# GpSimd's unread write behind every second scatter of x, two small steps on ScalarE, and new places in a fused attention and expert kernel

## The chip, the cores and the metric

One core of one Trainium2 chip. The metric is the device time of one execution, in microseconds (us), as the median of several runs. Engines are named as in the profile: PE (TensorE's matmuls), PEld (its weight loads), DVE (VectorE), ACT (ScalarE), POOL (GpSimd), SP (SyncE, which issues most of the DMAs).

## What is computed

An attention over channels, then a layer of experts over its output. Cut to what matters:

```python
# q, k, v: (4, 5056, 256); attention between the 256 channels of a batch
qn = q / (norm(q, axis=1) + 1e-06)
kn = k / (norm(k, axis=1) + 1e-06)
a = softmax(kn.transpose(0, 2, 1) @ qn / tau)        # (4, 256, 256)
x = (v @ a).reshape(20224, 256)
# experts: tokens with x @ w_skip > 0 go to the expert with the largest logit
e_idx = argmax(xc @ w_gate); gate_w = softmax(xc @ w_gate)[e_idx]      # 8 experts
y[mask_e] = gate_w * (relu(xc[mask_e] @ w1[e]) @ w2[e])                # 256 -> 1024 -> 256
out = x;  out[do_compute] = xc + y
```

## The kernel before

The tokens of a batch are cut into 4 chunks of 1280 (10 groups of 128), so there are 16 chunks, numbered c or d from 0 to 15. The work of one TensorE runs through these stages, which overlap:

- **Scores** (`scores`, L734, matmul L743): for chunk c, ten steps that add `k^T q` of 128 tokens into a PSUM tile of the batch. Meanwhile ScalarE squares q and k (L714) and VectorE adds the squares up (`add_squares`, L718) for the norms. The `qk` tiles are loaded in halves of a chunk, with 5 buffers.
- **Softmax** (`softmax`, L746), once a batch, behind its fourth chunk of scores: copy of the sums, norms by matmuls with ones (L730), square root, reciprocal, exponent (L772), then `aug` = exponent x 1 / sum (L778, VectorE), transposes of `aug` on TensorE (L783), the product with the gate's weights (L791), and the split of `aug` into `aH` and `aL` (L797, L799).
- **Product** (`attend`, L803, matmuls L815 to L817): for chunk d, five steps of two groups each into one of two pairs of PSUM banks (`px`). ScalarE copies each step out (`keep_x`, L821): `xo` (L824) holds x, `lg` (L825) holds the ten logits. `xo` has three buffers (`NXO`), so the first copy of chunk d waits until the scatters and the store of chunk d - 3 have landed.
- **Routing** (`route`, L839) of chunk d, from `lg`: maximum and difference (VectorE), exponent (`r_ex`, L853, ScalarE), the one-hot of the expert and its running count (L856 to L865, VectorE), the counts per partition as `r_rc` (L868, VectorE), two matmuls that sum them over the partitions (L871, L872, TensorE), `r_before` (L875, ScalarE), then offsets and places (`r_off` L883 to `r_posi` L894, VectorE). `base` carries the counts from chunk to chunk.
- **Scatter** (L897, GpSimd): ten indirect DMAs a chunk, each writing 128 rows of `xo` (x, token number, gate weight) to their places in `srt`, a list in DRAM sorted by expert. Behind each stands `pace` (L648): a memset of a tile `idle` that nothing reads (L650). The scatters of all chunks form one chain in GpSimd's order. `end_lists` (L657) closes the lists with four more scatters (L671) that have no memset between them.
- **First experts** (`first_ahead`, `second_ahead`): 7 blocks of 512 tokens of one expert, from the scatters of the first 6 chunks (`D0`), multiplied between and behind the products of the last chunks. `xs` and `xg` are their rows, loaded from `srt`; `put_ahead` scatters the result to `out` (L236, GpSimd).
- **Small slots** (`Small.part`), one after the other with the rest of the first experts, then two loops over what is left (`Large.loop`, L460; `Small.loop`, L602), whose code is no part of the change. The loop of large slots runs from about 502 us to the end.

The order of every engine up to the loops is made by a planner (`Plan`, L61): each step is a task with an engine, a cost, dependencies and a due time. Due times come from a table, `PLACES` (L51): two numbers for each chunk of scores (A), each chunk of products (B), each block of first experts (H) and each small slot (S). `run` (L109) hands due times back along the dependencies, simulates the engines and sorts the tasks by start; the program is written out in that order, and each engine keeps it. Costs are numbers such as `("G", 3.5)`: GpSimd's two scatters with their memsets.

Of the kernel before, what the change touches and what calls it, by code (L numbers as in the profile page):

```python
# [48 lines left out]
NXO = 3  # L49

PLACES = """  # L51
A0 89.87 855.42, A1 390.44 1819.31, A2 -81.94 1047.65, A3 -59.52 1015.95, A4 -190.99 1534.08, A5 -120.99 1138.75, A6 499.15 783.13, A7 799.47 1506.97, 
A8 1050.89 1421.23, A9 298.20 825.70, A10 1109.61 1383.20, A11 632.60 1820.36, A12 403.39 543.02, A13 425.18 1096.75, A14 1034.62 1129.27, A15 429.61 1087.73, 
B0 1339.22 1377.19, B1 -184.38 1551.63, B2 716.25 1563.50, B3 81.23 1352.19, B4 1080.02 1305.66, B5 743.88 863.60, B6 558.44 1600.08, B7 1608.33 1676.51, 
B8 288.55 958.87, B9 -0.98 1608.03, B10 259.38 1309.95, B11 174.32 789.24, B12 1048.96 1138.93, B13 919.54 2739.02, B14 949.98 1651.89, B15 178.90 1291.75, 
H0 672.92 1892.93, H1 231.51 1144.86, H2 169.77 1607.46, H3 1140.58 1342.54, H4 671.59 905.84, H5 257.88 1165.77, H6 1054.77 1575.39, S0 517.30 1920.36, 
S1 491.32 1739.07, S2 822.24 1425.79, S3 270.07 987.21, S4 568.78 659.45, S5 1154.04 1192.59, S6 1621.29 1716.68, S7 1357.86 1445.79
"""


class Plan:  # L61
# [18 lines left out]
    def chain(self, gen, *steps, deps=(), due=1e9):  # L80

        ts = []
        for engine, cost in steps:
            ts.append(self.add(engine, cost, lambda: next(gen, None), [*deps, *ts[-1:]], due))
            deps = ()
        return ts
# [90 lines left out]
def attn_moe(ctx: ExitStack, tc: tile.TileContext, q_k, vt, tau, w_skip, w_gate, w1, w1q, w2, out):  # L177
# [470 lines left out]
    def pace():  # L648

        G.memset(idle, 0.0)  # L650
# [95 lines left out]
    def softmax(b):  # L746


        u = pb.tile([P, 2, C], F32, name="u")
        S.copy(u, sums[b])  # L750
        yield
        add_norms(b)
        yield
        m = norms[b]
        nrm = pb.tile([P, C + 4], F32, name="nrm")
        V.tensor_scalar(nrm, m[:, : C + 4], 1e-30, None, ALU.max)
        yield
        S.activation(nrm, nrm, AF.Sqrt)
        yield
        V.tensor_scalar(nrm, nrm, 1e-6, None, ALU.add)  # L760
        V.reciprocal(nrm, nrm)
        rk = pb.tile([P, 2], F32, name="rk")
        V.tensor_scalar(rk, nrm[:, C : C + 4 : 2], itau, None, ALU.mult)
        yield
        mx = pb.tile([P, 2], F32, name="mx")
        den = pb.tile([P, 2], F32, name="den")
        for cb in range(2):
            V.scalar_tensor_tensor(u[:, cb, :], u[:, cb, :], rk[:, cb : cb + 1], nrm[:, :C], ALU.mult, ALU.mult)
        V.tensor_reduce(mx, u, AX.X, ALU.max, negate=True)
        yield  # L770
        for cb in range(2):
            S.activation(u[:, cb, :], u[:, cb, :], AF.Exp, bias=mx[:, cb : cb + 1], accum_out=den[:, cb : cb + 1])  # L772
        yield
        V.tensor_scalar(den, den, 1e-9, None, ALU.add)
        V.reciprocal(den, den)
        aug = pb.tile([P, 2, NA], F32, name="aug")
        for cb in range(2):
            V.tensor_scalar(aug[:, cb, :C], u[:, cb, :], den[:, cb : cb + 1], None, ALU.mult)  # L778
        yield
        pt = ps_m.tile([P, 2, C], F32, name="m")  # L780
        for cb in range(2):
            for kb in range(2):
                T.transpose(pt[:, kb, cb * P : (cb + 1) * P], aug[:, cb, kb * P : (kb + 1) * P], ident)  # L783
        yield
        aT = u
        S.copy(aT, pt)
        yield
        pw = ps_m.tile([P, 512], F32, name="m")
        for cb in range(2):
            for kb in range(2):  # L790
                T.matmul(pw[:, cb * 10 : cb * 10 + 10], aT[:, kb, cb * P : (cb + 1) * P], w9[:, kb, :], start=(kb == 0), stop=(kb == 1), skip_group_check=True)  # L791
        yield
        V.tensor_copy(aug[:, :, C:], pw[:, :20].rearrange("p (c e) -> p c e", c=2))
        yield
        aH = pb.tile([P, 2, NA], F32R, name="aH", bufs=2)
        aL = pb.tile([P, 2, NA], F32R, name="aL", bufs=2)
        S.copy(aH, aug)  # L797
        yield
        V.tensor_tensor(aL, aug, aH, ALU.subtract)  # L799
        augs[b] = (aH, aL)  # L800
        yield
# [37 lines left out]
    def route(d):  # L839
# [25 lines left out]
        V.tensor_tensor_scan(inc, segm, oh.rearrange("p e t -> p (e t)"), 0.0, ALU.mult, ALU.add)  # L865
        inc = inc.rearrange("p (e t) -> p e t", e=E)
        rc = tile_([P, E], "r_rc", F32R)
        V.tensor_copy(rc, inc[:, :, n - 1 : n].rearrange("p e o -> p (e o)"))  # L868
        yield
        m = ps_m.tile([P, 512], F32, name="m")  # L870
        T.matmul(m[:, :E], tri_r, rc, start=True, stop=True, skip_group_check=True)  # L871
# [24 lines left out]
        for t in range(n):  # L896
            i = G.indirect_dma_start(  # L897
                out=srt, out_offset=IndirectOffsetOnAxis(ap=posi[:, t : t + 1], axis=0),
                in_=xos[d][:, t, :], in_offset=None, bounds_check=E * CAP - 1, oob_is_err=False)
            in_list(i)  # L900
            if d >= D0:
                beside(i, "later lists", "first lists")
            else:
                first_listed.append(i.ins.name)
            pace()
            if t % 2:
                yield

    def tables(start):
# [83 lines left out]
    for c in range(NC):  # L993
        b, ch = divmod(c, NCH)
        ld, users = {}, ([], [])
        for h in range(2):
            cuts = {(0, 0): (0, 1, 2, 3, 4, JH), (0, 1): (0, 2, JH), (1, 0): (0, 2, JH)}.get((c, h), (0, JH))
            for j0, j1 in zip(cuts, cuts[1:]):
                t = then("qk", add("D", 0.68 * (j1 - j0), lambda c=c, h=h, j0=j0, j1=j1: load_qk(c, h, j0, j1), due=1e9 if c else -99, hold=("part", 99) if j0 else ("qk", NQ)))
                t.users = [] if j0 else users[h]  # L1000
                ld.update((h * JH + j, t) for j in range(j0, j1))
        for n in range(2):
            for h in range(2):
                begins = ch == 0 and h == 0
                s0 = then(("sq", n), add("S", 1.18, lambda c=c, n=n, h=h: squares(c, n, h), [ld[j] for j in range(h * JH, (h + 1) * JH)], hold=None if begins else ("sqh", 3)))
                users[h].append(s0)
                if begins:
                    if b:
                        s0.deps.append(ready_a[b - 1, "n"])
                    summed[n] = s0  # L1010
                else:
                    summed[n] = add("V", 1.41, lambda c=c, n=n, h=h: add_squares(c, n, h), [s0, summed[n]])
                    s0.users = [summed[n]]
            if ch == NCH - 1:
                summed[n] = add("V", 1.53, lambda n=n: fold_squares(n), [summed[n]])
        g = scores(c)
        for j in range(J):
            deps = [ld[j]]
            if j == 0 and ch == 0 and b > 1:
                deps.append(freed_s[b - 2])  # L1020
            t = then("A", add("T", 0.865, lambda g=g: next(g), deps, at("A", c, j)))
            if j % JH == JH - 1:
                users[j // JH].append(t)
        last_a = t
        if c == 2:
            third = t
        if ch == NCH - 1:
            g = softmax(b)
            s0, = chain(g, ("S", 0.5), deps=[t])
            n0, = chain(g, ("T", 0.8), deps=[s0, summed[0], summed[1]])  # L1030
            s = chain(g, ("V", 0.36), ("S", 1.65), ("V", 2.3), ("V", 1.55), ("S", 2.35), ("V", 0.97), deps=[n0])
            m0, = chain(g, ("T", 0.45), deps=s[-1:])
            m1, = chain(g, ("S", 0.5), deps=[m0])
            m2, = chain(g, ("T", 0.9), deps=[m1])
            m3, = chain(g, ("V", 0.12), deps=[m2])
            aH, = chain(g, ("S", 0.55), deps=[m3])
            aL, = chain(g, ("V", 0.65), deps=[aH])
            m0.hold = m2.hold = ("m", 1)
            m0.users, m2.users = [m1], [m3]
            freed_s[b], ready_a[b], ready_a[b, "n"] = s0, aL, n0  # L1040
            if b:
                s0.deps.append(ready_a[b - 1])
            norms_read = s[0]
# [8 lines left out]
    for d in range(NC):  # L1052
# [22 lines left out]
        stored[d] = then("st", add("D", 3.4, lambda d=d: store(d), [s], at("B", d, 4, by=16.5)))  # L1075
        g = route(d)
        r = chain(g, ("V", 0.43), deps=[s] + ([routed[d - 1]] if d else []))
        r += chain(g, ("S", 0.17), ("V", 1.02), ("V", 0.46), deps=r)
        rt, = chain(g, ("T", 0.22), deps=r[-1:])
        ra, = chain(g, ("S", 0.07), deps=[rt])  # L1080
        rt.hold, rt.users = ("m", 1), [ra]
# [1 line left out]
        routed[d], = chain(g, ("V", 0.51), deps=[based[d]])  # L1083
        routed[d].due = at("B", d, 4, by=2)
        s0.users = [routed[d]]
        in_order["sc"] = chain(g, *[("G", 3.5)] * (J // 2), deps=[routed[d], in_order.get("sc")], due=at("B", d, 4, by=15 if d < D0 else 45))[-1]
        sorted_[d] = plan.landed(in_order["sc"], 4.3)
        if d == NC - 1:
            g = end_lists()
# [202 lines left out]
```

## Time and profile before

| | |
|---|---|
| median of 3 runs | 778.78 us (778.5 to 779.02) |
| the profiled execution | 777.67 us |
| its span, first to last instruction | 775.9 us |
| TensorE busy in the span | 740.7 us |
| VectorE, ScalarE, GpSimd busy | 519.7, 346.8, 369.9 us |
| mean granted clock of TensorE | 0.986 |

The profiled execution is one run with its own time; its rows give durations and waits, and the span is 1.8 us shorter than its time. In the page, a matmul's end is modelled, so an engine that is shown busy may hold short waits. The idle time of an engine matters only where a later step of the bounding engine waits for it. In rows of groups, "x160 | 189.0, 1181 | 102.3 <-..." is: how many, busy us in all, mean ns of one, idle us before them and what ended it.

### The profile page before, as it was taken

The page shows a single profiled execution, that of the slowest core. Times are in us where ns is not written, and L with a number is a line of the kernel's source. Part 1 is how long each engine was busy: PE and PEld are TensorE (multiplying, and loading weights), DVE is VectorE, ACT ScalarE, POOL GpSimd, SP SyncE. Part 2 cuts the span into 40 slices and gives each one's busy share as a digit, 9 for nine tenths or more (in the row PEclk, how much of TensorE's full clock was granted, in tenths as well). Part 3 has the DMA queues.
Part 4 walks back from the last instruction along what each step waited for, and adds up shares of the span by engine and source line. Part 5 has one row for each costly group of instructions (what it writes and reads, how often), then busy time and mean ns, then how long its engine had stood idle before and what let it go on. Part 6 is the DMA issues. An engine that isn't in the chain of part 4 may idle for free. (4 is left out here: it accounts for less than half of the span.)

```text
span 775.9 us, 13511 instructions
## 1 busy us (share of the span) xinstructions
PE 740.7 (95%) x4352; PEld 643.9 (83%) x4352; DVE 519.7 (67%) x995; ACT 346.8 (45%) x605; POOL 369.9 (48%) x450
## 2 busy tenths in 40 slices
PE   9989999698999699999997999999999999999996
PEld 8879998698988688899886677788888888888885
DVE  3877959695887597777983425266657576666755
ACT  4678648545863655343230314143434243434422
POOL 1000899999999998889864130311122211111122
PEclk9999999899999899999999999999999999999998
DMA  8999998799958737466369996252533425152441
GB/s 323 398 390 342 357 353 289 259 333 378 353 194 238 213 116 230 134 218 161 132 216 296 305 382 234 79 184 75 167 97 108 135 73 178 60 183 75 129 117 54
DMA packets 97651, 165.98 MB, mean 214 GB/s; under 512 B 50650, under 2 KB 75460, under 8 KB 89280
## 3 DMA queue, kind: packets, MB, share of 16 engines
q1 hardware_dynamic: 85136, 144.03, 55.8%
q0 software_dynamic: 11776, 21.31, 7.9%
q8 instruction: 26, 0.43, 0.2%
q14 instruction: 25, 0.20, 0.1%
q10 hardware_dynamic: 688, 0.01, 0.0%
HBM read 122.26 MB, written 53.92 MB: 227 GB/s over the span
## 5 line engine op out<-in xcount | busy, mean ns | idle before, releaser
L897 POOL DMA_INDIRECT srt<-xo,r_posi x160 | 189.0, 1181 | 102.3 <-ACT sqh L714 73.5
L236 POOL DMA_INDIRECT out<-xg x76 | 76.1, 1001 | 251.9 <-DVE xg L371 227.4
L743 PE MATMUL s<-qk 128*128 128x256 f32 x640 | 146.8, 382 | 2.6 <-DMA qk<-in_qk 2.6
L743 PEld LDWEIGHTS s<-qk 128*128 128x128 f32 x640 | 118.9, 191 | 18.2 <-DMA qk<-in_qk 3.8
L815 PE MATMUL px<-aH,vH 128*128 128x266 f32 x320 | 98.7, 309 | 14.8 <-ACT lg L825 14.6
L344 DVE SCALAR_TENSOR_TENSOR hL<-ph,hH 128x512 fp32r<-128x512 f32 x96 | 66.4, 691 | 58.9 <-ACT hH L343 57.6
L343 ACT ACTIVATE hH<-ph 128x512 fp32r<-128x512 f32 x96 | 57.4, 598 | 98.0 <-PE ph L340 98.0
L816 PE MATMUL px<-aL,vH 128*128 128x266 f32 x320 | 92.9, 290 | 0.9 <-DVE aL L799 0.9
L817 PE MATMUL px<-aH,vL 128*128 128x266 f32 x320 | 92.7, 290 | 0.0
L650 POOL MEMSET none<- 128x512 bf16 x160 | 88.7, 554 | 0.0
L363 PE MATMUL po<-w2s,hH 128*128 128x512 f32 x336 | 83.8, 391 | 0.0
L824 ACT COPY xo<-px 128x512 f32<-128x512 f32 x80 | 47.2, 591 | 69.8 <-PE px L817 36.9
L815 PEld LDWEIGHTS px<-aH,vH 128*128 128x128 f32 x320 | 61.8, 193 | 17.3 <-ACT lg L825 16.2
L338 PE MATMUL ph<-xH,w1H 128*128 128x512 f32 x192 | 74.9, 390 | 0.9 <-PE m L1175 0.9
L339 PE MATMUL ph<-xL,w1H 128*128 128x512 f32 x192 | 74.8, 390 | 0.0
L340 PE MATMUL ph<-xH,w1L 128*128 128x512 f32 x192 | 74.7, 389 | 0.0
L714 ACT ACTIVATE sqh<-qk 128x1280 f32<-128x1280 f32 x56 | 69.3, 1273 | 9.2 <-DMA qk<-in_qk 4.8
L363 PEld LDWEIGHTS po<-w2s,hH 128*128 128x128 f32 x336 | 61.2, 189 | 11.5
L307 ACT CAST xH<-xt 128x512 fp32r<-128x512 f32 x40 | 24.9, 623 | 90.4 <-DVE xt L305 90.4
L816 PEld LDWEIGHTS px<-aL,vH 128*128 128x128 f32 x320 | 62.0, 194 | 2.3 <-DVE aL L799 1.4
L371 DVE SCALAR_TENSOR_TENSOR xg<-po,xg 128x256 f32<-128x256 f32 x90 | 43.5, 483 | 30.1 <-PE po L365 28.6
L817 PEld LDWEIGHTS px<-aH,vL 128*128 128x128 f32 x320 | 61.6, 192 | 0.0
(184 smaller groups left out, 1351.1 us busy)
## 6 DMA issues: line engine op xcount, KB each, us to landing
qk<-in_qk SPq DMA_DIRECT2D x29, 1280.0 KB
vf<-in_vt SPq DMA_DIRECT2D x32, 640.0 KB
out<-xo SPq DMA_DIRECT2D x12, 1280.0 KB
xg<-srt SPq DMA_DIRECT2D x20, 516.0 KB, 3.3
xs<-srt SPq DMA_DIRECT2D x80, 128.0 KB, 3.2
v1r<-in_w SPq DMA_DIRECT2D x10, 1024.0 KB
v2r<-in_w SPq DMA_DIRECT2D x10, 1024.0 KB
w1r<-in_w1q SPq DMA_DIRECT2D x8, 1024.0 KB, 5.5
```

What stands on the lines that cost most here:

```text
L236: i = (G.indirect_dma_start(out=out, out_offset=IndirectOffsetOnAxis(ap=ls, axis=0), in_=src, in_offset=None, bounds_check=NTOK - 1, oob_i ...
L338: T.matmul(ph, self.w1H[:, fs], self.xH[:, kb, :], start=(kb == 0), stop=False)
L339: T.matmul(ph, self.w1H[:, fs], self.xL[:, kb, :], start=False, stop=False)
L340: T.matmul(ph, self.w1L[:, fs], self.xH[:, kb, :], start=False, stop=(kb == 1))
L363: yield T.matmul(po, self.hH[:, f, ts], self.w2s[:, f, :, :], start=(f == 0), stop=False, skip_group_check=True)
L650: G.memset(idle, 0.0)
L714: S.activation(to, qk[c, h][:, n], AF.Square)
L743: T.matmul(sums[b][:, cb, :], kt[:, j % JH, cb * P : (cb + 1) * P], qt[:, j % JH, :], start=(ch == 0 and j == 0 and cb == 0), stop=(ch == ...
L815: T.matmul(px[:, i, :NA], vH[:, kb, js], aH[:, kb, :], start=(kb == 0), stop=False)
L816: T.matmul(px[:, i, :NA], vH[:, kb, js], aL[:, kb, :], start=False, stop=False)
L817: T.matmul(px[:, i, :NA], vL[:, kb, js], aH[:, kb, :], start=False, stop=(kb == 1))
L897: i = G.indirect_dma_start(out=srt, out_offset=IndirectOffsetOnAxis(ap=posi[:, t : t + 1], axis=0), in_=xos[d][:, t, :], in_offset=None, b ...
```

## The change

`pace()` moves inside the test for every second scatter, so that a chunk of ten scatters has five memsets. In `route`, `r_rc` is copied by ScalarE and not by VectorE. In `softmax`, the two multiplications that make `aug` run on ScalarE (an activation with a scale for each partition) and not on VectorE. Each of the two steps becomes a task of its own, with a cost in the planner, and the cost of GpSimd's pair of scatters goes from 3.5 to 3.4. The 47 pairs of `PLACES` are all new; their numbers are due times and say little one by one.

```diff
 PLACES = """
-A0 89.87 855.42, A1 390.44 1819.31, A2 -81.94 1047.65, A3 -59.52 1015.95, A4 -190.99 1534.08, A5 -120.99 1138.75, A6 499.15 783.13, A7 799.47 1506.97, 
...
+A0 -212.84 779.51, A1 1321.85 2287.98, A2 1288.02 1918.41, A3 921.83 1283.14, A4 -211.85 1066.57, A5 1.96 1135.44, A6 1521.56 1748.04, A7 866.77 2427.61, 
...
@@ softmax
         V.reciprocal(den, den)
+        yield
         aug = pb.tile([P, 2, NA], F32, name="aug")
         for cb in range(2):
-            V.tensor_scalar(aug[:, cb, :C], u[:, cb, :], den[:, cb : cb + 1], None, ALU.mult)
+            S.activation(aug[:, cb, :C], u[:, cb, :], AF.Copy, scale=den[:, cb : cb + 1])
@@ route
         rc = tile_([P, E], "r_rc", F32R)
-        V.tensor_copy(rc, inc[:, :, n - 1 : n].rearrange("p e o -> p (e o)"))
+        yield
+        S.copy(rc, inc[:, :, n - 1 : n].rearrange("p e o -> p (e o)"))
...
-            pace()
             if t % 2:
+                pace()
                 yield
@@ costs in the planner
-            s = chain(g, ("V", 0.36), ("S", 1.65), ("V", 2.3), ("V", 1.55), ("S", 2.35), ("V", 0.97), deps=[n0])
+            s = chain(g, ("V", 0.36), ("S", 1.65), ("V", 2.3), ("V", 1.55), ("S", 2.35), ("V", 0.35), ("S", 0.75), deps=[n0])
-        r += chain(g, ("S", 0.17), ("V", 1.02), ("V", 0.46), deps=r)
+        r += chain(g, ("S", 0.17), ("V", 1.02), ("V", 0.33), ("S", 0.18), deps=r)
-        in_order["sc"] = chain(g, *[("G", 3.5)] * (J // 2), deps=[routed[d], in_order.get("sc")], due=at("B", d, 4, by=15 if d < D0 else 45))[-1]
+        in_order["sc"] = chain(g, *[("G", 3.4)] * (J // 2), deps=[routed[d], in_order.get("sc")], due=at("B", d, 4, by=15 if d < D0 else 45))[-1]
```

Lines behind the changed ones move down by one to two (L897 becomes L899, L824 becomes L825, L853 becomes L854, L875 becomes L877; `r_rc` is L870, `aug` L779). Two places of the order follow; numbers behind a name tell one buffer's use from another.

GpSimd, at the end of the chain of scatters, where the last rows of chunk 15 are followed by the closing scatters. Before:

```order
L650 MEMSET none_143 128x512
L897 DMA srt_88<-xo_3753,r_posi_4077 167424x258
L650 MEMSET none_143 128x512
L668 CAST endi_4213<-ends_4209 128x4
L671 DMA srt_88<-none_143,endi_4213 167424x258 x4
```

Now:

```order
L650 MEMSET none_143 128x512
L899 DMA srt_88<-xo_3755,r_posi_4004 167424x258 x2
L650 MEMSET none_143 128x512
L668 CAST endi_4137<-ends_4133 128x4
L671 DMA srt_88<-none_143,endi_4137 167424x258 x4
```

Scatters stand in pairs with one memset behind them. The closing scatters stand without one, as before.

ScalarE, from the last product step of chunk 4 to the first of chunk 5, which is the first copy into the `xo` buffer that chunk 2 held. Before (`xo_1369` is chunk 5, `r_ex_1387` and `r_before_1463` are the routing of chunk 4):

```order
L824 COPY xo_1241<-px_1331 128x2x256
L825 COPY lg_1271<-px_1331 128x20
L700 CAST vH_1365<-vf_1163 128x1280
L714 ACTIVATE sqh_1388<-qk_1029 128x1280
L853 ACTIVATE r_ex_1387<-r_d_1385 128x80
L824 COPY xo_1369<-px_1370 128x2x256
L825 COPY lg_1406<-px_1370 128x20
L824 COPY xo_1369<-px_1392 128x2x256
L825 COPY lg_1406<-px_1392 128x20
L714 ACTIVATE sqh_1444<-qk_1188 128x1280
L875 COPY r_before_1463<-m_1447 128x16
```

Now (`xo_1441` is chunk 5; `r_ex_1388`, `r_rc_1414` and `r_before_1439` are the routing of chunk 4):

```order
L825 COPY xo_1268<-px_1359 128x2x256
L826 COPY lg_1289<-px_1359 128x20
L700 CAST vH_1382<-vf_1126 128x1280
L854 ACTIVATE r_ex_1388<-r_d_1386 128x80
L714 ACTIVATE sqh_1400<-qk_1191 128x1280
L714 ACTIVATE sqh_1410<-qk_1191 128x1280
L870 CAST r_rc_1414<-r_inc_1412 128x8
L714 ACTIVATE sqh_1429<-qk_1238 128x1280
L877 COPY r_before_1439<-m_1431 128x16
L714 ACTIVATE sqh_1464<-qk_1238 128x1280
L825 COPY xo_1441<-px_1442 128x2x256
L826 COPY lg_1470<-px_1442 128x20
```

All three ScalarE steps of the routing of chunk 4 now stand ahead of the first copy of chunk 5; before, `r_before` stood behind it.

## Rows read from the trace of the kernel before

**Rows 1.** The page, part 1: busy us, share of the span, instructions.

```profile
PE 740.7 (95%) x4352; PEld 643.9 (83%) x4352; DVE 519.7 (67%) x995; ACT 346.8 (45%) x605; POOL 369.9 (48%) x450
```

**Rows 2.** The waits, whole span: who waited for whom, us in total, times, longest.

```profile
ACT xo L824 <- DMA srt<-xo,r_posi: 31.7, 7, 7.4
...
PE px L815 <- ACT lg L825: 14.6, 4, 6.7
...
PE px L338 <- DVE xg L371: 4.3, 1, 4.3
```

**Rows 3.** The timeline of PE: start, us, instruction, idle before it and what ended it.

```profile
145.79 0.59 PE L815 MATMUL px<-aH,vH 128*128 128x266 f32 x1 [6.00 <-ACT lg L825]
...
265.56 0.59 PE L815 MATMUL px<-aH,vH 128*128 128x266 f32 x1 [6.70 <-ACT lg L825]
```

**Rows 4.** The timeline of ACT at the same two places.

```profile
145.07 0.59 ACT L824 COPY xo<-px 128x512 f32<-128x512 f32 x1 [6.25 <-DMA srt<-xo,r_posi]
...
264.84 0.59 ACT L824 COPY xo<-px 128x512 f32<-128x512 f32 x1 [6.13 <-DMA srt<-xo,r_posi]
```

**Rows 5.** The timeline of POOL: scatters of chunks 2, 4, 8 and 9.

```profile
129.58 2.10 POOL L897 DMA_INDIRECT srt<-xo,r_posi  x1 [0.17 <-issue]
...
137.68 0.98 POOL L897 DMA_INDIRECT srt<-xo,r_posi  x1 [0.17 <-DVE r_mx L848]
...
159.61 0.97 POOL L897 DMA_INDIRECT srt<-xo,r_posi  x1 [0.16 <-ACT sqh L714]
...
257.91 0.97 POOL L897 DMA_INDIRECT srt<-xo,r_posi  x1 [0.16 <-DVE xt L305]
...
259.59 0.99 POOL L897 DMA_INDIRECT srt<-xo,r_posi  x1 [0.17 <-issue]
```

**Rows 6.** Windows: us, busy us of PE, PEld, DVE, ACT, POOL, granted clock, DMA share, GB/s.

```profile
78.00:259.00 181.00, 169.83 (x1038) 155.65 (x1036) 140.69 (x286) 111.36 (x193) 165.93 (x180) 0.98 0.86 305
```

**Rows 7.** Windows, line L650 (the unread write) alone: us, busy POOL.

```profile
78.00:259.00 181.00, 49.52 (x90) 0.98 0.86 305
```

**Rows 8.** Windows, line L897 (the scatters) alone: chunk 2, and chunks 0 to 8.

```profile
116.00:139.00 23.00, 16.29 (x10) 1.00 0.84 272
78.00:259.00 181.00, 117.64 (x90) 0.98 0.86 305
```

**Rows 9.** The timeline of DVE: two adds, two steps of chunk 4's routing.

```profile
129.35 1.48 DVE L718 TENSOR_TENSOR sqk<-sqk,sqh 128x1280 f32<-128x1280 f32 x1
...
137.88 1.48 DVE L705 TENSOR_TENSOR vL<-vf,vH 128x1280 fp32r<-128x1280 f32 x1
...
149.27 0.17 DVE L883 TENSOR_TENSOR r_off<-r_before,base 128x8 f32<-128x8 f32 x1 [5.63 <-ACT r_before L875]
...
150.52 0.17 DVE L894 SCALAR_TENSOR_TENSOR r_posi<-r_pos,r_mx 128x10 int32<-128x10 f32 x1
```

**Rows 10.** The timeline of POOL: the closing scatters.

```profile
397.16 0.99 POOL L671 DMA_INDIRECT srt<-none,endi  x1 [4.11 <-DMA xs<-srt]
398.45 0.98 POOL L671 DMA_INDIRECT srt<-none,endi  x1 [0.30 <-issue]
```

**Rows 11.** Windows, behind the second and the third gap of TensorE.

```profile
266.00:269.00 3.00, 3.00 (x14) 2.90 (x14) 2.49 (x6) 2.56 (x8) 2.67 (x4) 0.50 0.34 75
423.00:426.00 3.00, 3.00 (x8) 2.33 (x8) 2.56 (x5) 0.00 (x0) 2.17 (x3) 0.50 1.02 389
```

**Rows 12.** The timeline of DVE behind the third gap.

```profile
420.53 0.23 DVE L424 TENSOR_SCALAR xg<-xg,nobody 128x4 int32<-128x4 int32 x1 [11.22 <-DMA xg<-srt]
```

**Rows 13.** Groups by line: out<-in, shapes, count, busy us, mean ns, idle before.

```profile
L743 PE MATMUL s<-qk 128*128 128x256 f32 x640 | 146.8, 382 | 2.6 <-DMA qk<-in_qk 2.6
...
L868 DVE CAST r_rc<-r_inc 128x8 fp32r<-128x8 f32 x16 | 5.1, 321 | 0.8
...
L772 ACT ACTIVATE u<-u,mx 128x256 f32<-128x256 f32 x8 | 4.0, 499 | 0.2
L778 DVE TENSOR_SCALAR aug<-u,den 128x256 f32<-128x256 f32 x8 | 4.0, 538 | 0.1
```

More of the change, by code (lines that the diff above doesn't have):

```diff
@@ L51 @@
 PLACES = """
-A0 89.87 855.42, A1 390.44 1819.31, A2 -81.94 1047.65, A3 -59.52 1015.95, A4 -190.99 1534.08, A5 -120.99 1138.75, A6 499.15 783.13, A7 799.47 1506.97,
[L53 to L57, printed above, removed]
+A0 -212.84 779.51, A1 1321.85 2287.98, A2 1288.02 1918.41, A3 921.83 1283.14, A4 -211.85 1066.57, A5 1.96 1135.44, A6 1521.56 1748.04, A7 866.77 2427.61,
+A8 1669.19 1909.96, A9 1529.84 1745.34, A10 49.51 1125.18, A11 964.56 1241.96, A12 76.13 775.39, A13 1533.28 1646.93, A14 284.14 322.32, A15 605.99 1645.34,
+B0 -553.38 1624.65, B1 1059.41 1229.58, B2 1324.08 2043.89, B3 774.09 2431.92, B4 187.89 1016.60, B5 1367.03 1932.84, B6 157.71 569.73, B7 202.72 464.71,
+B8 855.77 2530.12, B9 1438.10 1858.11, B10 1153.34 1832.22, B11 1096.41 1886.67, B12 777.75 2410.50, B13 798.41 1410.74, B14 1275.11 2037.27, B15 1124.02 1912.70,
+H0 756.73 1449.91, H1 1567.64 1958.30, H2 211.59 521.38, H3 380.89 734.47, H4 1225.45 2144.35, H5 297.48 436.13, H6 1041.42 1976.08, S0 1664.16 1808.51,
+S1 1589.25 1784.53, S2 1183.50 2100.39, S3 491.56 743.28, S4 317.74 323.84, S5 1044.45 2181.99, S6 1496.20 1816.03, S7 1625.43 1829.53
 """
```

## The prediction

> **What bounds the kernel now.** I read the page first. TensorE is busy 95% of the span [rows 1], so only its gaps can be won; I then looked for who ends them. The waits by engine show one family: TensorE stood 14.6 us for ScalarE's copies out of PSUM, and ScalarE's `xo` copies stood 31.7 us for the scatters of x [rows 2]. The PE timeline gives the two large gaps, 6.00 us before 145.79 and 6.70 us before 265.56 [rows 3]. At the same places the ScalarE timeline has the first copy of a chunk waiting 6.25 and 6.13 us for a scatter to land [rows 4]. By the code that copy is of chunk 5, then of chunk 11, and what it needs is a free one of three `xo` buffers: the scatters of chunk 2 and of chunk 8. On GpSimd the last scatter of chunk 2 ends at 138.66 and the last of chunk 8 at 258.88 [rows 5]; the copies start 6.4 and 6.0 us later. So from 78 to 259 us a chain on GpSimd sets the pace: 90 scatters, one after another, then about 6 us of landing. GpSimd is busy 165.93 of those 181 us [rows 6].
>
> That chain has three parts. A scatter takes 0.97 us at least. The unread write behind it takes 49.52 / 90 = 0.55 us [rows 7]. The rest is a wait: 117.64 / 90 = 1.307 us is the mean scatter [rows 8], 0.337 over the floor. The DVE timeline tells what it is. The scatter at 129.58 took 2.10 us [rows 5]; an add of two SBUF tensors had begun at 129.35 and ran to 130.83 [rows 9], 1.25 us into it. The scatter at 137.68 began ahead of an add (137.88) and took 0.98. A scatter that starts beside a running add of two SBUF inputs waits for its end, then needs 0.85.
>
> **The change, term by term.** The sum is made against the profiled execution (777.67 us), 1.1 below the median of the runs, 778.78.
>
> 1. *Half of the unread writes go.* With one, the next scatter starts 259.59 - 257.91 = 1.68 us after the last [rows 5]. Without one, the closing scatters into `srt` start 398.45 - 397.16 = 1.29 us apart [rows 10]: the engine idles 0.30 there instead of 0.17, so a write costs 0.39 net, not 0.55. Ahead of the landing of chunk 8 there are 90 scatters; 45 writes go: 45 x 0.39 = **17.6 us**. As GpSimd sets this chain, the copy of chunk 11 comes 17.6 earlier, and TensorE with it. Bounds: if TensorE becomes the bound first, it can give its idle time of 78 to 259 us, 181 - 169.83 = 11.2 [rows 6], the gap of 6.7 behind it and some 1.5 for the three microseconds after it at a granted clock of 0.50, the 1.2 GHz level [rows 11]: 19.4 at most. At the other end, if each pulled-forward scatter met an add and lost the 0.39 again, nothing is won. I take 17.6, with the wait per scatter as it is in the rows, because how much of the time such adds run on VectorE doesn't depend on GpSimd's writes.
>
> 2. *Behind chunk 8* 35 more writes go (35 x 0.39 = 13.7 us of GpSimd). I cost them at nothing. From there GpSimd starts a chunk when its routing is done, and that follows TensorE. What stands behind is the third gap, 4.3 us of TensorE for VectorE's `xg` [rows 2]: VectorE waited 11.22 us for an `xg` load [rows 12], that load for the puts of `xg`, these for the closing scatters, and those, 4.11 us idle, for the `xs` loads [rows 10]. The `xs` loads follow TensorE's pace, so this chain moves with it and the gap stays. If it went, it would give 4.3 and some 1.5 of half clock [rows 11], 5.8: the low end.
>
> 3. *Two small steps to ScalarE.* `aug` was 538 ns x 2 per softmax on VectorE, `r_rc` 321 ns x 16 [rows 13]: 8 x 0.54 + 16 x 0.32 = 9.4 us off VectorE. On ScalarE the nearest row is 499 ns for a 128x256 activation [rows 13], which an 8-column cast won't exceed: at most 24 x 0.5 = 12 us, over the whole run, on an engine busy 111 of these 181 us [rows 6]. On the path: nothing. For `aug` the cover is the scores that TensorE computes between the norms and the transposes; in the PE order of batch 1 that grows from 8 to 13 steps of scores and from 3 to 4 of the product. If that cover were gone, a hop and a step would cost under 1 us a batch. `r_rc` is now queued behind ScalarE's own waits, which is the routing rival below.
>
> 4. *New places.* TensorE's work is the same; only its order moves. Before, ScalarE's `r_before` of chunk 4 stood behind the copy that waited for chunk 2, and VectorE's `r_off` waited 5.63 us for it [rows 9]. Now the three ScalarE steps of that routing stand ahead of the copy. Against that, the PE order puts 101 steps of scores, not 94, ahead of the end of chunk 4's product, 7 x 146.8 / 160 = 6.4 us more [rows 13]. So chunk 4 is routed at about 150.69 - 5.6 + 6.4 = 151.5 [rows 9], and GpSimd, which began it at 159.61 [rows 5], is free for it at 159.61 - 20 x 0.39 = 151.8. A tie: cost 0. DMA engines were busy a share of 0.86 at 305 GB/s in the stretch [rows 6]; the same bytes 17.6 us sooner ask 338, under the 389 that another stretch reached [rows 11].
>
> Sum: 777.67 - 17.6 = 760.1; as a median, 1.1 more: **761.2 us**.
>
> A rule that speaks against the change: the Trainium skill, SBUF — State Buffer, section Who interferes with whom, says that a VectorE instruction with two SBUF inputs contends with a GpSimd instruction that reads SBUF, not with one that only writes it. The trace agrees: adds stretch scatters [rows 5, 9], and the writes average 0.55 us [rows 7]. By it the unread write is time in which an add runs out unharmed, and by it alone each of 45 scatters pulled forward could lose the 1.13 us of the one at 129.58: 51 us, less 17.6, some 33 us slower at worst, where the rows' mean wait makes it 17.6 faster.
>
> **The rivals.**
>
> *The waits grow (slower).* A scatter pulled forward starts into an add that the write would have let pass. Price: the break-even is 17.6 / 90 = 0.195 us more wait per scatter, 0.53 instead of 0.337. In chunk 2, where the adds stand back to back, the mean was 1.63 us [rows 8], 0.66 over the floor. If all nine chunks came to that: 90 x 0.32 = 29 longer, less 17.6: +11.5, **790**. For it: VectorE is busy 141 of 181 us [rows 6], and a shorter stretch packs its adds closer. Against it: GpSimd starts as many scatters against as many adds as before.
>
> *Routing becomes the bound (gain, but less).* If ScalarE reaches `r_rc` of chunk 3 to 5 late, GpSimd waits for the list. If the 5.6 us of term 4 don't come free, it idles 5.6: 17.6 - 5.6 = 12, **767**. For it: the tie above, and a third ScalarE step in each routing.
>
> *Both chains get shorter.* The scatter waits shrink, TensorE becomes the bound, and the third gap closes: 777.67 - 19.4 - 5.8 + 1.1 = **754**. For it: the writes' share of GpSimd's time falls. Against: term 2.
>
> *The queue drains no faster.* If scatters can't be taken at 1.29 us, each second one grows by 0.39 and nothing changes: **779**. Against it: the closing scatters ran at 0.30 us idle with no longer spans [rows 10].
>
> **How the numbers follow.** Chances: the forecast 0.56, routing 0.18, both shorter 0.12, waits grow 0.09, no faster drain 0.05. The likeliest case gives 761.2. The range takes in the first three: low 752, a little under 754 for idle time that the trace's busy TensorE hides; high 771, which is 761.2 plus half of the 17.6 given back. That leaves out the last two and the tails. About 0.2% is what a measurement of this kernel can tell from no change; faster 0.86, same 0.05, slower 0.09.
>
> **What would show it.** Right: 80 unread writes; scatters that follow each other at 1.29 and 1.68 us in turn; a mean scatter near 1.31 us up to the landing of chunk 8; the last scatter of that chunk near 241 us; no TensorE gap at chunk 5, one of up to 6 us at chunk 11; the third gap still there, some 18 us earlier; the loop unchanged. Wrong: a mean scatter above 1.5 us; GpSimd idle for `r_posi` in chunks 3 to 6; ScalarE's `xo` copy waiting as long as before; TensorE waiting on `qk` loads; a new gap at a softmax.

## The result and the profile after

| | before | after |
|---|---|---|
| median | 778.64 us (776.45 to 779.02, 4 runs) | 753.54 us (751.94 to 755.6, 4 runs) |
| ratio, with its 95% interval | | 0.9685 (0.9654 to 0.9716) |
| the profiled execution, its span | 777.67, 775.9 us | 751.94, 750.1 us |
| mean granted clock of TensorE | 0.986 | 0.997 |

Faster by 25.1 us: inside the range (752 to 771), but 7.7 us below the forecast of 761.2, and within half a microsecond of the rival in which both chains get shorter (754), which is chance, as the account below shows. The profiled execution of the changed kernel is the shortest of its four, with a mean granted clock of 0.997 where the other three have 0.995, so that what follows of its clock isn't shown for those.

The page, part 1 (busy us, share of the span, instructions), against [rows 1]:

```profile
PE 733.9 (98%) x4352; PEld 638.6 (85%) x4352; DVE 504.1 (67%) x971; ACT 351.7 (47%) x629; POOL 328.6 (44%) x370
```

GpSimd has 80 instructions fewer (the writes), and 24 steps went from VectorE (995 to 971) to ScalarE (605 to 629). The waits, against [rows 2]:

```profile
POOL srt L671 <- DMA xs<-srt: 9.2, 1, 9.2
...
PE px L338 <- DVE xg L371: 2.8, 1, 2.8
ACT xo L825 <- DMA srt<-xo,r_posi: 2.5, 2, 1.4
...
PE px L816 <- ACT lg L826: 1.5, 1, 1.5
```

ScalarE's wait for the scatters fell from 31.7 to 2.5 us and TensorE's for ScalarE's copies from 14.6 to 1.5. The third gap is still there, 2.8 us instead of 4.3. The closing scatters wait longer than before, 9.2 us and not 4.1: GpSimd is done with chunk 15 sooner and waits for the `xs` loads all the same.

The windows (us; busy us of PE, PEld, DVE, ACT, POOL; granted clock, DMA share, GB/s), against [rows 6, 11]: first the stretch up to the landing of chunk 8, then three microseconds behind each of TensorE's two gaps.

```profile
78.00:242.00 164.00, 164.00 (x1029) 152.87 (x1029) 129.73 (x270) 113.98 (x205) 142.17 (x136) 1.00 0.94 334
...
245.00:248.00 3.00, 2.62 (x17) 2.18 (x16) 2.34 (x8) 2.70 (x8) 2.53 (x4) 1.00 1.03 333
...
398.00:401.00 3.00, 2.89 (x12) 2.17 (x12) 2.92 (x6) 0.00 (x0) 2.25 (x3) 1.00 0.94 366
```

TensorE, idle for 11.2 of 181 us before, is busy in all 164. Behind neither gap did the clock fall in this execution; before, it was at 0.50 behind both. The window of the scatters alone, chunks 0 to 8:

```profile
78.00:240.10 162.10, 116.84 (x90) 1.00 0.94 334
```

116.84 / 90 = 1.298 us is the mean scatter, 1.307 before [rows 8]. The POOL timeline has the new pattern, the last scatter of chunk 8 (at 237.88) and the first closing one:

```profile
226.96 0.98 POOL L899 DMA_INDIRECT srt<-xo,r_posi  x1 [0.17 <-issue]
228.24 0.98 POOL L899 DMA_INDIRECT srt<-xo,r_posi  x1 [0.30 <-issue]
229.20 0.55 POOL L650 MEMSET none<- 128x512 bf16 x1
229.92 1.51 POOL L899 DMA_INDIRECT srt<-xo,r_posi  x1 [0.17 <-issue]
...
237.88 2.14 POOL L899 DMA_INDIRECT srt<-xo,r_posi  x1 [0.30 <-issue]
...
374.00 0.99 POOL L671 DMA_INDIRECT srt<-none,endi  x1 [9.22 <-DMA xs<-srt]
```

Starts are 1.28 us apart without a write, 1.68 with one. The last scatter of chunk 8 ends at 240.02, against 258.88. ScalarE's first copy of chunk 11, against [rows 4], from its timeline:

```profile
243.79 0.59 ACT L825 COPY xo<-px 128x512 f32<-128x512 f32 x1 [1.17 <-PE px L818]
```

And TensorE's timeline at the two gaps that are left, and at the start of the loop of large slots:

```profile
244.50 0.39 PE L816 MATMUL px<-aH,vH 128*128 128x266 f32 x1 [1.49 <-ACT lg L826]
...
398.11 0.47 PE L338 MATMUL px<-xH,w1H 128*128 128x512 f32 x1 [2.78 <-DVE xg L371]
...
477.51 0.47 PE L338 MATMUL ph<-xH,w1H 128*128 128x512 f32 x1 [0.92 <-PE m L1177]
```

The same two rows of the kernel before, the third gap and the loop:

```profile
422.73 0.68 PE L338 MATMUL px<-xH,w1H 128*128 128x512 f32 x1 [4.30 <-DVE xg L371]
...
503.17 0.47 PE L338 MATMUL ph<-xH,w1H 128*128 128x512 f32 x1 [0.91 <-PE m L1175]
```

So the 25.7 us of the two profiled executions add up along the way: 18.9 where chunk 8's last scatter ends, 21.1 at chunk 11's first copy (264.84 to 243.79), 24.6 behind the third gap, 25.7 at the loop, which itself is unchanged (775.9 - 503.2 = 272.7 before, 750.1 - 477.5 = 272.6 after). By the page, TensorE's idle time went from 775.9 - 740.7 = 35.2 to 16.2 us, and its busy time, for the same 4352 matmuls, from 740.7 to 733.9.

### The profile page after: what moved, and what is told of

It is laid out like the page before. It is cut to its first block, busy times and chain, and to the rows that moved or that the text cites. A ratio compares the mean times of both kernels' runs of the same rounds, so it can differ in the third digit from the quotient of the medians.

```text
span 750.1 us, 13405 instructions
## 1 busy us (share of the span) xinstructions
PE 733.9 (98%) x4352; PEld 638.6 (85%) x4352; DVE 504.1 (67%) x971; ACT 351.7 (47%) x629; POOL 328.6 (44%) x370
## 5 line engine op out<-in xcount | busy, mean ns | idle before, releaser
L899 POOL DMA_INDIRECT srt<-xo,r_posi x160 | 190.9, 1193 | 115.2 <-ACT sqh L714 73.5
L816 PE MATMUL px<-aH,vH 128*128 128x266 f32 x320 | 97.1, 303 | 1.5 <-ACT lg L826 1.5
L825 ACT COPY xo<-px 128x512 f32<-128x512 f32 x80 | 47.1, 591 | 52.8 <-PE px L818 48.6
L363 PE MATMUL px<-w2s,hH 128*128 128x512 f32 x216 | 57.6, 398 | 0.0
```

What stands on the lines that cost most here:

```text
L363: yield T.matmul(po, self.hH[:, f, ts], self.w2s[:, f, :, :], start=(f == 0), stop=False, skip_group_check=True)
L816: T.matmul(px[:, i, :NA], vH[:, kb, js], aH[:, kb, :], start=(kb == 0), stop=False)
L899: i = G.indirect_dma_start(out=srt, out_offset=IndirectOffsetOnAxis(ap=posi[:, t : t + 1], axis=0), in_=xos[d][:, t, :], in_offset=None, b ...
```

## The experiments

E1 and E7 edit the kernel before, all others the changed kernel. Medians are of 4 to 6 runs and ratios are to the kernel before on the same chip (776.38 to 777.46 us), unless it says one run. "Chunk 8" is the time in the profile at which its last scatter ends; "third gap" that of TensorE for `xg`. Both come from one profiled execution, which in E2 (771.0 us), E5 (754.5) and E9 (774.7) was the longest of its kernel.

| | median, us | ratio (95%) | chunk 8 | third gap |
|---|---|---|---|---|
| before | 778.64 | 1 | 258.9 | 4.30 |
| after | 753.54 | 0.9685 (0.9654 to 0.9716) | 240.0 | 2.78 |
| E1 half the writes only | 757.22 | 0.9734 (0.9706 to 0.9762) | 234.8 | 4.01 |
| E2 new order, all writes | 766.73 | 0.9844 (0.9813 to 0.9876) | 249.6 | 4.44 |
| E3 old places | 764.37 | 0.9821 (0.9794 to 0.9849) | 240.6 | 3.73 |
| E4 small steps back on VectorE | 759.01 | 0.9753 (0.9724 to 0.9783) | 235.6 | 5.02 |
| E5 no writes | 753.09 | 0.9689 (0.9665 to 0.9713) | 227.0 | 4.46 |
| E6 two writes behind each pair | 792.28 | 1.0182 (1.0146 to 1.0218) | 264.7 | 7.06 |
| E7 = E1, small steps on ScalarE | 758.14 | 0.9758 (0.9736 to 0.9781) | 237.6 | 3.61 |
| E8 closing scatters free | 749.12 | 0.9648 (0.9626 to 0.967) | 240.3 | none |
| E9 new places alone | 771.47 | 0.9915 (0.9882 to 0.9948) | 252.5 | 4.03 |
| E10 most adds of squares left out | 753.11 (1 run) | | 231.5 | 4.02 |
| E11 the write reads SBUF | 763.4 (1 run) | | 243.9 | 4.52 |
| E12 = E8, no writes | 747.23 | 0.962 (0.9597 to 0.9642) | 226.7 | none |

### E1: half of the writes, nothing else

```diff
-            pace()
             if t % 2:
+                pace()
                 yield
```

> The kernel before with one edit: the unread write behind every second scatter. Orders of all other engines stay as before. Theory P (GpSimd's chain sets the pace up to the landing of chunk 8, a write costs 0.39 us net): the last scatter of chunk 8 ends near 241 us, the copy of chunk 11 starts near 247, and the time is 757 to 763 us. Theory O (the gain is in the new places, which take TensorE past its wait at chunk 5): that wait of 6 us mostly stays and the time is 772 us or more.

757.22 us, in the range of theory P: 20.2 of the 25.1 come from the writes alone. Chunk 8 is done at 234.8, 5 us sooner than in the changed kernel, and TensorE waits neither at chunk 5 nor at chunk 11 for more than half a microsecond; yet the end is 3.7 us later. What is left of TensorE's waits for ScalarE's copies in E1:

```profile
PE px L815 <- ACT lg L825: 0.5, 1, 0.5
```

The scatters take 111.8 us here, 5.8 less than before, so more than the writes was won. From here on GpSimd is not the bound, and the rest of the change does something that GpSimd doesn't show.

### E2: the new order and the steps on ScalarE, with all writes

```diff
+            pace()
             if t % 2:
-                pace()
                 yield
```

> The changed kernel with the unread write back behind each scatter; new places and ScalarE's two steps stay. Theory P: the last scatter of chunk 8 ends near 258 us again, TensorE waits some 17 us in front of chunk 11 or earlier, and the time is 772 to 782 us. Theory O: 755 to 764 us.

766.73, in neither theory's range: without touching a write, 10.7 us come from the order and the two steps. Chunk 8 is done at 249.6, 9.3 sooner than before: the 90 scatters up to there take 107.9 us and not the 117.6 of [rows 8]. By the two traces 29 of them start beside a running add of 128x1280, and 36 did before. Halving the writes then brings 13.2 (766.73 to 753.54), and E1's 20.2 where it is done alone. The parts don't add.

### E3: the old places

```diff
 PLACES = """
...
-A0 -212.84 779.51, A1 1321.85 2287.98, A2 1288.02 1918.41,
+A0 89.87 855.42, A1 390.44 1819.31, A2 -81.94 1047.65,
...
```

> The changed kernel with the table of places of before: halved writes and ScalarE's two steps stay, the order is made from the old due times. Theory P: 754 to 762 us. Theory O: 770 us or more, with TensorE's wait at chunk 5 back.

764.37, in neither theory's range. Chunk 8 is done at 240.6, as in the changed kernel, and still the end is 10.8 us later. The waits of TensorE in E3:

```profile
PE px L338 <- DVE xg L371: 5.3, 2, 3.7
PE ph L338 <- issue: 3.5, 1, 3.5
PE m L873 <- ACT r_rc L870: 2.5, 2, 2.3
```

With the old due times the planner puts one `r_rc` on ScalarE where TensorE waits 2.3 us for it; the waits for `xg` are 5.3 us and not 2.8; and at the start of the loop of large slots TensorE stands 3.5 us, for which the profile names no cause, where the changed kernel has 0.92. The other parts need the new places: "cost 0" for them was wrong.

### E4: the two small steps back on VectorE, TensorE's order unchanged

```diff
-            S.activation(aug[:, cb, :C], u[:, cb, :], AF.Copy, scale=den[:, cb : cb + 1])
+            V.tensor_scalar(aug[:, cb, :C], u[:, cb, :], den[:, cb : cb + 1], None, ALU.mult)
...
-        S.copy(rc, inc[:, :, n - 1 : n].rearrange("p e o -> p (e o)"))
+        V.tensor_copy(rc, inc[:, :, n - 1 : n].rearrange("p e o -> p (e o)"))
```

> The changed kernel with the multiplications of aug and the cast of r_rc back on VectorE, in the places that ScalarE's steps have now; TensorE's order is the same. Theory P (the small steps lie beside other work): within 2 us of the changed kernel, 752 to 757 us. Theory S (relief of VectorE carries a part of the gain): 759 us or more.

5.5 us slower than the changed kernel, though chunk 8 is done 4.4 us sooner. The waits of TensorE in E4:

```profile
PE px L338 <- DVE xg L371: 5.0, 1, 5.0
PE m L873 <- DVE r_rc L870: 3.2, 6, 1.0
```

In the changed kernel no wait for `r_rc` is left in this view; before, it was 2.4 us:

```profile
PE m L871 <- DVE r_rc L868: 2.4, 3, 1.6
```

The DVE timeline of E4 has what `r_rc` stands behind at one of these waits, and the PE timeline the wait:

```profile
230.33 1.47 DVE L705 TENSOR_TENSOR vL<-vf,vH 128x1280 fp32r<-128x1280 f32 x1
231.71 0.17 DVE L870 CAST r_rc<-r_inc 128x8 fp32r<-128x8 f32 x1
...
231.93 0.27 PE L873 MATMUL m<-r_rc,tri_r 128*128 128x8 f32 x1 [0.61 <-DVE r_rc L870]
```

The step is short, the add ahead of it in VectorE's order is not. Four of the six waits, 1.6 of the 3.2 us, come behind such an add; the longest, 1.04, comes behind steps of a softmax, among them a reciprocal of 1.78 us, and one of 0.53 behind a step of the first experts. In the profiled executions the third gap begins 2.8 us later than in the changed kernel, although the 1.5 us at chunk 11 are gone; it is 2.2 longer; and the stretch from it to the loop takes 1.9 more, at a granted clock of 0.50 up to 407.2. That is 6.9 us between these two executions, and 5.5 between the medians. So the waits for `r_rc` explain a part of the loss, and the third gap and the clock are more than half of it; why the gap got longer was not taken apart.

### E5: no writes at all

```diff
             if t % 2:
-                pace()
                 yield
```

> The changed kernel without any unread write. Theory P with TensorE now the bound: GpSimd's chain gets another 45 x 0.41 = 18 us shorter up to chunk 8, but TensorE has only the 1.5 us gap left in front of chunk 11, so the time is 751 to 754 us. If GpSimd still set the pace, it would be 740 us or less; if the scatters' waits for VectorE's adds grow when nothing stands between them (the slower rival), 757 us or more, with a mean scatter above 1.45 us.

753.09, no gain over 753.54, with chunk 8 done 13 us sooner. TensorE no longer waits at chunk 11, reaches the third gap 1.5 us sooner, and stays there that much longer. The PE timeline of E5, against 398.11 in the changed kernel:

```profile
398.33 0.77 PE L338 MATMUL px<-xH,w1H 128*128 128x512 f32 x1 [4.46 <-DVE xg L371]
```

What ends the third gap comes at 398 in both. The other half of the writes is hidden, and the third gap takes what TensorE won.

### E6: as many writes as before, but two behind each pair

```diff
             if t % 2:
                 pace()
+                pace()
                 yield
```

> The changed kernel with two unread writes behind every second scatter: as many as before the change, in pairs. If what counts is the time that the writes take on GpSimd, the pair of scatters takes 0.97 + 0.30 + 0.97 + 1.10 + 0.2 = 3.5 us and the time is 763 to 770 us, as with a write behind each (766.7). If what counts is the spacing of the scatters, the time stays at 752 to 756 us.

792.28, 25.6 us slower than E2, which has the same number of writes, and slower than the kernel before: neither expectation came. Its POOL timeline:

```profile
124.14 0.97 POOL L899 DMA_INDIRECT srt<-xo,r_posi  x1 [0.29 <-ACT sqh L714]
125.42 0.97 POOL L899 DMA_INDIRECT srt<-xo,r_posi  x1 [0.30 <-issue]
126.38 1.13 POOL L650 MEMSET none<- 128x512 bf16 x2
127.80 1.47 POOL L899 DMA_INDIRECT srt<-xo,r_posi  x1 [0.29 <-ACT aH L798]
```

A pair takes 127.80 - 124.14 = 3.66 us; two scatters with a write behind each take 2 x 1.68 = 3.36 [rows 5]. Over 45 pairs that is 13.5 us; the scatters take 110.1 us, 2.2 more than in E2; and chunk 8 is done at 264.7, 15.1 later than in E2. That end again orders the times: 249.6 and 766.7, 252.5 and 771.5 (E9), 258.9 and 778.6, 264.7 and 792.3. It isn't the whole of E6's loss: between chunk 11 and the end of the third gap another 7.7 us come, among them a wait of 3.8 for VectorE's `hL` and 2.6 more in the third gap.

### E7: E1 with the two small steps on ScalarE, in E1's order of TensorE

The two lines of E4 the other way round, on top of E1's edit.

> The kernel before with the writes halved (757.2 us) and aug and r_rc on ScalarE, each in the slot of the VectorE instruction that it replaces; TensorE's order is that of before. If the small steps take load off VectorE and that is worth 5 us wherever they stand: 751 to 754 us. If their worth in the changed kernel is that TensorE's order waits for r_rc behind VectorE's adds there: 756 to 759 us here, where TensorE waits less than 2 us for r_rc.

758.14 against 757.22: nothing won. TensorE's waits for `r_rc` were 1.0 us in E1 and are 1.0 here, for ScalarE now. The step from VectorE to ScalarE is worth its 5 us only in the new order.

### E8: the closing scatters no longer wait for the `xs` loads

The closing scatters write the rows behind the end of each list and the `xs` loads of the first blocks read other rows; E8 says so to the program, which then keeps no order between them.

```diff
             in_list(i)
+            beside(i, "later lists", "first lists")
             if k % 2:
                 yield
```

> The changed kernel with the four closing scatters declared free of the loads of the first experts' rows, which lie elsewhere in the lists. If the third gap is the chain xs loads, closing scatters, puts, xg load (term 2): the closing scatters start at 365 instead of 374 us, the gap of 2.8 us closes and no stretch at half clock follows: 749 to 752 us. If the gap is the slow landing of the xg load between weight loads: the gap stays and the time is 752 to 755 us.

749.12, 4.4 us faster than the changed kernel and faster than all kernels above (2.8 between the two profiled executions). The POOL timeline of E8:

```profile
364.80 0.26 POOL L668 CAST endi<-ends 128x4 int32<-128x4 f32 x1
365.33 0.99 POOL L671 DMA_INDIRECT srt<-none,endi  x1 [0.28 <-POOL endi L668]
366.63 0.97 POOL L671 DMA_INDIRECT srt<-none,endi  x1 [0.30 <-issue]
```

The first closing scatter starts at 365.33 and not at 374.00, and TensorE's wait for `xg` is gone. The load of `xg` lets VectorE go on at 392.45 and not at 395.92. This shows that the closing scatters' wait for the `xs` loads makes the third gap, as the prediction read it. The links behind it (puts of `xg`, load, VectorE, TensorE) are read from the order and the waits; that the load came only 3.5 us sooner, where the closing scatters came 8.7 sooner, was not taken apart.

### E9: the new places alone

E2's and E4's edits together: only the order is new.

> New places and the planner's new steps alone: an unread write behind each scatter, aug and r_rc on VectorE. With ScalarE's steps it was 766.7 us. If the new order by itself spares the scatters part of their waits for VectorE's adds (20.6 us of waits up to chunk 8 there, 31.4 in the kernel before): 764 to 772 us, the last scatter of chunk 8 between 247 and 254 us. If it was the relief of VectorE: 774 us or more, chunk 8 ending near 258 us.

771.47, 5.4 us faster than before; chunk 8 is done 6.4 us sooner, since its and the earlier scatters take 110.9 us and not 117.6. (The waits before were 117.6 - 90 x 0.97 = 30.3 us, not the 31.4 of the expectation.) Against E2 the steps are worth 4.7 us here as well, but along another way: chunk 8 is done 2.9 us later than there, and TensorE's waits for `r_rc` are 1.6 us in all.

### E10: most of the adds of squares left out

The squares of the first 640 tokens are scaled up and the adds shortened from 1280 to 8 columns, so the norms are approximate; everything else is computed.

```diff
-        S.activation(to, qk[c, h][:, n], AF.Square)
+        S.activation(to, qk[c, h][:, n], AF.Square, scale=2.81 if to is sqs[n] else 1.0)
...
-        V.tensor_tensor(sqs[n], sqs[n], sqh.pop((c, n, h)), ALU.add)
+        V.tensor_tensor(sqs[n][:, 0, :8], sqs[n][:, 0, :8], sqh.pop((c, n, h))[:, 0, :8], ALU.max)
```

> The changed kernel without most of VectorE's adds of squares: the norms are taken from the first 640 tokens of each batch with a scale, and 56 adds of 128x1280 shrink to 8 columns. If a scatter's length over 0.97 us is its wait for a running add of two SBUF inputs: the mean scatter of chunks 0 to 8 falls from 1.30 to 1.05 to 1.12 us, what the 18 adds of vL leave. If it is the DMA queues that hold it: it stays at 1.25 or more, as the traffic stays the same.

The window of the scatters of chunks 0 to 8 in E10:

```profile
78.00:231.60 153.60, 99.64 (x90) 1.00 0.94 340
```

1.107 us a scatter, against 1.298: of 0.33 us over the floor of 0.97, 0.19 were these adds. The time didn't move (753.11), as in E5: the scatters were no longer the bound.

### E11: a write that reads

```diff
-        G.memset(idle, 0.0)
+        G.tensor_copy(idle[:, : 2 * P], ones.bitcast(mybir.dt.bfloat16))
```

> The changed kernel with the unread write turned into a copy of 256 bf16 from a constant tile: it reads SBUF. If VectorE's adds hold only GpSimd instructions that read SBUF: some of the 80 copies are stretched by up to 1.4 us, those that start inside an add, and the time is 754 to 760 us. If they hold the scatters for another reason: all copies have the same length within 0.1 us.

763.4, one run and above the expected range; chunk 8 is done 3.9 us later, and the first copy of chunk 11 starts 6.5 us behind that and not 3.8. The POOL timeline of E11 has two of its copies:

```profile
158.62 0.43 POOL L650 COPY none<-ones 128x256 bf16<-128x256 bf16 x1
...
161.48 1.58 POOL L650 COPY none<-ones 128x256 bf16<-128x256 bf16 x1
```

and the DVE timeline the add beside the second:

```profile
161.35 1.46 DVE L705 TENSOR_TENSOR vL<-vf,vH 128x1280 fp32r<-128x1280 f32 x1
```

Of the 45 copies ahead of that landing, 25 took 0.41 to 0.55 us, and none of those met an add of 128x1280 that was running when it started. The other 20 all did, and took 0.82 to 1.58. The memsets of the changed kernel took 0.55 to 0.59 throughout. Here the Trainium skill's rule that the prediction weighed (SBUF — State Buffer, section Who interferes with whom) holds: a VectorE instruction with two SBUF inputs holds up a GpSimd instruction that reads SBUF, not one that only writes it. The same section of the Trainium skill also infers that `tensor_tensor` doesn't hold up GpSimd's work on DMAs, as this needs only the write side. E10 and [rows 5, 9] say otherwise of these scatters: 2.10 us beside a running add, 0.98 without.

### E12: E8 without writes

E5's and E8's edits together.

> Both at once: no unread writes, closing scatters free of the first experts' loads. TensorE is the bound up to the third gap, and that gap is closed: 746 to 749 us, 1 to 2 us under the 749.1 of the free closing scatters with half of the writes. If scatters without writes harm the loads: 750 us or more.

747.23, the fastest, 5.9 us below E5. Now the rest of the writes is worth something, 1.9 us against E8: TensorE's 1.5 us at chunk 11 are gone and the third gap isn't there to take them.

## Why the prediction was right, and where it was off

**What bounds the kernel: right.** GpSimd's chain up to the landing of chunk 8 set the pace. The five kernels in which chunk 8 is done later than 243 us stand in the order of that time, from E11 to E6.

**Term 1, half of the writes, 17.6: right in mechanism.** A write cost 0.39 net: 45 of them are 17.6, the scatters took 0.8 less, and the end of chunk 8 came 18.9 sooner, at 240.02 where 241 was said. The rival of growing waits fell: the mean scatter was 1.298 us, not 1.63. That it stayed at the 1.31 of before is luck, and not for the reason given, that "GpSimd starts as many scatters against as many adds as before": 41 of the 90 start beside a running add, not 36, but the add then has 0.79 us left in the mean, not 0.98. In the other orders the mean was 1.243 (E1), 1.199 (E2) and 1.232 (E9). With the other parts as before (E1) the writes won 20.2, and chunk 8 ended at 234.8.

**What term 1 left out: the landing and the clock.** From the last scatter's end to the copy it was 6.0 us, now it is 243.79 - 240.02 = 3.8 at most, which gives 2.2. The step that failed is "the copy of chunk 11 comes 17.6 earlier, and TensorE with it": it took the landing to be as long as before. And the bound of 19.4 counted the half clock behind the second gap only. Behind the first it had fallen too, as a window of the kernel before shows:

```profile
146.00:149.00 3.00, 3.00 (x15) 3.00 (x15) 0.00 (x0) 1.47 (x3) 2.67 (x5) 0.50 1.07 412
149.00:152.00 3.00, 3.00 (x23) 3.00 (x23) 2.28 (x8) 2.56 (x6) 2.83 (x4) 0.88 0.21 75
```

At 0.50, the 1.2 GHz level, three microseconds cost 1.5, and at 0.88 another 0.4, an estimate from the clock of these rows: TensorE was "busy" there and had 1.9 us to give. The windows behind the three gaps hold 1.9 + 1.5 + 1.5 = 4.9 [rows 11] of the 6.8 by which TensorE's busy time fell.

**Term 2, the third gap: the chain right, its size off.** "This chain moves with it and the gap stays": it stayed, at 2.78. But the load of `xg` moved by 24.6 us [rows 12] and not by 18, and TensorE by 23.1, so the gap lost 1.5, and the stretch at half clock behind it went, another 1.0. The row in the changed kernel:

```profile
395.92 0.23 DVE L424 TENSOR_SCALAR xg<-xg,nobody 128x4 int32<-128x4 int32 x1 [9.80 <-DMA xg<-srt]
```

If it had gone, 5.8 was the price given; E5 against E12 measured 5.9. Of the rival of both chains shorter, only parts came: TensorE became the bound but for 1.5 us at chunk 11, the scatters' waits shrank by 0.8 us in all, and the third gap got shorter but didn't close. That the time is its 754 is chance.

**Term 3, the small steps, "on the path: nothing": wrong.** They are worth 5.5 us (E4 against the changed kernel) and 4.7 with all writes (E9 against E2). I looked for the cover of `aug` and for a delay of `r_rc` on ScalarE, but not for what `r_rc` cost where it was: TensorE's waits had a row of 2.4 us for it. Of these, 1.6 are one wait in which the count ahead of `r_rc` had itself only just ended, so the row alone would have said too much. It is also a term that only its place makes: in the order before, it is worth nothing (E7). Which of the two steps carries how much was not run: only `r_rc` shows in TensorE's waits.

**Term 4, the places, 0: wrong both ways.** Alone they bring 5.4 us (E9), by shorter waits of the scatters; taken out of the changed kernel they cost 10.8 (E3). The tie in chunk 4's routing was set at 0 rightly: its list was ready at 147.2 and GpSimd began it at 150.2, so the rival of 767 didn't come. What failed is the step "the wait per scatter as it is in the rows": the order sets which scatters meet an add, and how much of it is left.

**The sum.** Along the way it is 18.9 (chunk 8's end), 2.2 (landing), 2.0 from there to the third gap (the half clock behind the second gap among it), 1.5 (third gap) and 1.0 (clock behind it): 25.7 in the profiled executions, 25.1 in the medians. Alone, the parts bring 20.2 (writes), 5.4 (places) and, in the old order, nothing (steps); that this comes near the whole is chance, since E3 and E4 show each one's worth to depend on the others. The range's high end has a slip: 761.2 and half of 17.6 are 770, not 771, which decides nothing here.

Why the landing got shorter is open. The DMA engines' share was full in both stretches from the last scatter's end to the copy (1.05 before and after). These are their packets, before (258.88 to 264.84) and after (240.02 to 243.79):

```profile
DMA packets 2040, 1.72 MB, mean 288 GB/s; under 512 B 1282, under 2 KB 1837, under 8 KB 2040
...
DMA packets 970, 1.48 MB, mean 391 GB/s; under 512 B 66, under 2 KB 770, under 8 KB 970
```

Before, the queue of the scatters moved no packet from 256.8 to 262.2, while another queue took 98.8% of the engines' time, and most packets of the stretch are under 512 bytes; after, it moved 92 packets in its stretch, and few of all packets are that small. The landing was as short in E8 (3.8 us), and 6.5 to 7.9 us in E2, E6, E9 and E11, where the copy also waited for it. It may depend on where the chunk's end falls among the other transfers; no run took that apart.

## What to carry to other kernels

Price a delay by the work that stands behind it, not by the engine's busy time: here a write of 0.55 us cost 0.39 until TensorE was the bound and next to nothing after (45 of them 1.9 us in E12), and the gain of one chain showed up as a longer wait in the next (E5) until that one was cut too (E12). Before a small step on a busy engine is called free, look in the waits of the bounding engine for its name, and at each of them for what it stood behind. Moves of order and moves of work between engines must be tried together: the small steps were worth 5 us in the new order and nothing in the old.

## What the runs showed of the hardware that I had not expected

- Two memsets in a row cost more behind a scatter than one behind each of two (E6): the engine idles 0.29 us behind the pair of memsets and 0.17 behind a single one, and the spacing of scatters without one is 1.28, so the pair takes 3.66 and not 3.36 us.
- An add that holds up GpSimd is held up itself at times: beside E11's copies, adds of 128x1280 took up to 1.76 us instead of 1.48.
- Behind TensorE's gap of 2.78 us in the profiled execution of the changed kernel the granted clock stayed at 1.00. In every other kernel that has this gap it was 3.61 to 7.06 us, and the clock was at 0.50 for some 3 to 5.5 us behind it. From the gap's end to the loop it took 79.4 us in the changed kernel, 80.4 before, and 80.5 to 81.9 in E1, E2, E4, E5 and E7, so that a gap longer by one or two microseconds came with up to 2.5 more. What else differs between those stretches was not taken apart.
